# Two orders in a one-core attention and feed-forward kernel: the states' transposes against the tokens' sum, and the PSUM bank of one late product

## The chip, the core and the metric

The kernel runs on one NeuronCore of a Trainium2 chip. The metric is the device time of one execution in microseconds, as the median of several runs. The core has a matrix engine (TensorE; in profiles PE for matmuls and PEld for weight loads), VectorE (DVE), ScalarE (ACT), GpSimd (POOL) and SyncE (SP), which here issues the DMAs. Each engine works through a queue of its own in order and waits on semaphores for the others. SBUF is the working memory; PSUM holds the results of matmuls in eight banks of 128 partitions x 512 float32.

## What is computed

```python
def _attn_ref(x, state):                      # x: (8, 8, 512, 64), state: (8, 8, 32, 64)
    scores = scale * np.matmul(x, state.transpose(0, 1, 3, 2))
    a = softmax(scores)                       # written out: max, exp, sum + 1e-9
    xread = np.matmul(a, state)
    scores2 = scale * np.matmul(state, x.transpose(0, 1, 3, 2))
    a2 = softmax(scores2)
    sread = np.matmul(a2, x)
    return np.concatenate([xread, sread], axis=2)

def _moe_ref(x, w_in, w_out):                 # x: (8 * 544, 512)
    h = x @ w_in                              # 512 -> 2048
    g = h * (1.0 / (1.0 + np.exp(-1.702 * h)))
    return g @ w_out                          # 2048 -> 512
```

The weights of the feed-forward part arrive as float64 and are turned into float32 on the chip. Tokens read the states (`xread`), states read the tokens (`sread`), and the heads are laid side by side as the rows of the feed-forward part.

## The kernel before

The eight batches are handled one after the other. A batch's score products give two sets of exponentials: `e1`, the tokens' over the states, and `e2`, the states' over the tokens. The up product for tokens goes through M, which is the states times `w_in` (`att_M`, one part for each of four column chunks `c`), so that tokens' exponentials times M give `h` directly. The down product is a Strassen scheme of seven products, P1 to P7, each of which is in the middle batches itself a Strassen scheme of seven small ones; the small step `k` of product `P3` is called `P3.k`. VectorE forms the sums and differences that these schemes need, ScalarE copies banks out of PSUM and computes gelu.

The order of all work is written out by hand. While the down product of batch b runs, the attention of batch b + 1 is put between its steps: `hooks_next(b + 1)` fills a table from a step's name to functions, and `strassen_two` calls those of a step when that step's matmuls have been issued. Because every engine's queue is in order, the place in this table sets only the order within each engine. The table serves batches 2 to 7, the middle batches; batches 0 and 1 have their own order.

The piece of it that matters here runs around P3. `x_exp` (ScalarE) makes the tokens' exponentials, in two halves. `x_sum` (VectorE, L573) sums a half of them; `x_inverse` (L577, L578) follows when both sums are there. The states' exponentials `e2` leave for DRAM (`eT_out`) and come back in another layout (`eT_in`, one DMA of 512 KB hooked at P5, into the tile `eT`). `eT_turn(b, i)` (VectorE, L629) transposes one half of `eT` in place: i = 0 covers the head groups j = 0 and 1, i = 1 covers j = 2 and 3. Then `att_sread` (TensorE, L640, hooked at "run", after P3's last product) multiplies `eT` by the tokens, in 32 small matmuls whose innermost index is j. After it come `att_M` for chunks 3 and 2 (L456) and the product P7 (L820). The additions at L825 take a small product of P3 out of its PSUM bank; the first of the two that matter frees the bank into which P3's last small product writes.

At the start the order is another. Batch 0's up products f = 8 to 15 are issued late, by `up_late` through `up_x` and `up` (L673), because they need the last columns of `w_in`. The list `late_banks` gives four of them a bank of their own (`bank_o`). The others take the next bank of the pool `psH` (two buffers, tag "h"), unless `spare` is set, in which case they take the next of the pool `psA` (two buffers, tag "att"). A tile of a pool waits until the readers of the buffer's former tile are done: for `psH` here the gelu on ScalarE (L662). After these products come batch 0's and 1's first down product (L1551), M for batch 1, the states' reads of batches 1 and 0 (L640), an early up product of batch 1, and the down products of batch 0. Pieces of `w_out` are still being converted there: ScalarE clamps exponents (L225, L226), VectorE does the rest (L305 to L322).

The lines that a prediction has to follow in this place are:

```python
def eT_turn(b, i):
    t = A[b]["eT"][:, NG * i : NG * (i + 1)].rearrange("p j g q -> p (j g q)")
    nc.vector.transpose(t, t)

# att_sread: the order of the 32 products
for g in range(NG):
    for c in range(SCH):
        for j in range(NPR):
            e, v = a["eT"][:, j, g, Ns * c : Ns * (c + 1)], xn[b][:, NG * j + g, c]
```

Of the kernel before, what the change touches and what calls it, by code (L numbers as in the profile page):

```python
# [20 lines left out]
def kernel(  # L21
# [39 lines left out]
    NF = DF // P  # L61
# [537 lines left out]
    def att_M(b, c, spare=False, banks=None, copied=True):  # L599

        m = mpool.tile([P, NG, FC], FP32, tag=f"M{turns['M'] % NFC if b < 2 else c}", name=f"M_{b}_{c}")
        turns["M"] += 1
        A[b]["M", c] = m
        name = f"M_{b}_{c}_"
        ps = banks or [
            psH.tile([P, FC], FP32, tag="h", name=name + str(g)) if spare else att_ps([P, FC], name + str(g)) for g in range(NG)
        ]
        by_state(b, ps, lambda rows, j: w_in[c][rows, j])
        M_banks[b, c] = ps
        if copied:  # L610
            M_copies(b, c)
# [52 lines left out]
    def up(key, f, ntok, lhs, rhs, spare=False, bank=None, wait=False, dst=None):  # L664
        if bank is not None:
            hps = bank
        elif spare:
            hps = att_ps([P, ntok], f"h_{key}_{f}")
        else:
            hps = psH.tile([P, ntok], FP32, tag="h", name=f"h_{key}_{f}")  # L670
        n = len(lhs)
        for i in range(n):
            nc.tensor.matmul(hps, lhs[i], rhs[i], start=(i == 0), stop=(i == n - 1))  # L673
        if f % 2 == 0 and dst is None:
            G[key, f // 2] = free.pop(0)
        if dst is None:
            dst = G[key, f // 2][:, f % 2, :ntok]
        waiting.append((nc.scalar.activation, dict(out=dst, in_=hps, func=AF.Gelu_apprx_sigmoid)))
        if not wait:
            gelus(len(waiting))  # L680

    def up_x(b, f, spare=False, bank=None, wait=False, dst=None):
        c, o = divmod(P * f, FC)
        m = A[b]["M", c]
        up(b, f, S, [m[:, g, o : o + P] for g in range(NG)], [A[b]["aT"][:, g] for g in range(NG)], spare, bank, wait, dst)
# [375 lines left out]
    def hooks_next(b):  # L1061

        h = {}

        def at(name, fn, *args):
            h.setdefault(name, []).append((fn, args))

        def att_M1(b):
            att_M(b, 1, banks=[psH.tile([P, FC], FP32, tag="h", name=f"M_{b}_1_0"), bank_o[0]])

        first = b == 2
        p1, p2 = ("P1a", "P2a") if first else ("P1.2", "P1")
        at(p1, att_state, b)
        at(p2, att_scores, b)

        at("P2a" if first else "P2.1", load_x, b)
        at(p2, att_M, b, 0)
        if first:
            at(p2, att_M, b, 1, True)
        else:  # L1080
            at(p2, att_M1, b)
        at(p2, att_blocks, b)
        at("P2a" if first else "P2.1", att_s_max, b)
        p3 = "P2b" if first else "P2.3"
        at("P2a" if first else p3, att_s_exp, b)
        at(p3 if first else "P2", eT_out, b)
        steps = up_sums(b)

        A[b]["sums"] = {0: steps[9:11], 1: [steps[11], steps[14]]}
        if b == 2:  # L1090
            t0, t1, t2, t3 = ((turn_x, (b + 1, i)) for i in range(NPR))
            for i, v in enumerate([[], [t0, t1], [t2, t3]]):
                A[b]["sums"].setdefault(i, []).extend(v)
        elif b + 1 < B:
            for i in range(NPR):
                A[b]["sums"].setdefault(1 + i // 2, []).append((turn_x, (b + 1, i)))
        attention = [
            ("P6.1", att_s_norm), ("P6.1", x_max, 0), ("P6.2", x_sub, 0), ("P6.3", x_exp, 0), ("P6.6", x_max, 1),
            ("P3.1", x_sub, 1), ("P3.3", x_exp, 1), ("P3.4", x_sum, 0), ("P3.5", eT_turn, 0), ("P3.6", eT_turn, 1),
            ("P3.7", x_sum, 1), ("P3.7", x_inverse),  # L1100
            ("P5", eT_in), ("run", att_sread), ("run", att_M, 3, True), ("run", att_M, 2),
            ("T", x_scale, 0), ("T", x_scale, 1), ("P7.5", x_back, 0), ("P7.5", x_back, 1),
        ]
        names = {"P7.6": range(5), "P4.1": (5, 6), "P4.3": (7,), "P4.5": (8,), "P4.6": (12, 13)}
        for name, fn, *args in attention:
            at(name, fn, b, *args)
        for name, n in names.items():
            for i in n:
                at(name, steps[i][0], *steps[i][1])
        at("P7.2", att_srT, b)  # L1110
        return h


    def up_sums(b):

        a = A[b]

        def tt(out, x0, x1, op=ALU.subtract):
            nc.vector.tensor_tensor(out=out(), in0=x0(), in1=x1(), op=op)

        def rooms(step):
            if step == 0:
                t = apool.tile([P, NG, NB, Ns], FP32, tag="e1", name=f"ta_{b}").rearrange("p g i n -> p (g i n)")
                a["T"] = [t[:, QT * i : QT * (i + 1)] for i in range(4)]
            elif step == 1:
                t = apool.tile([P, NPR, S], FP32, tag="xT", name=f"ms_{b}")
                a["S1"], a["S2"] = t[:, :2], t[:, 2:]
            else:
                t = apool.tile([P, NG, SCH, P], FP32, tag="eT", name=f"m4_{b}")
                a["S4"] = t.rearrange("p g c q -> p g (c q)")  # L1130

        def T(i):
            return lambda: a["T"][i]

        def R(g, i):
            return lambda: a["aT"][:, g, QT * i : QT * (i + 1)]

        def M(c, g):
            return lambda: a["M", c][:, g]

        def V(name, c):
            return lambda: a[name][:, c]

        steps = [(rooms, (0,))]
        steps += [(tt, v) for v in ((T(0), R(0, 1), R(0, 0)), (T(2), R(1, 1), R(0, 1)), (T(1), R(1, 1), T(0)), (T(3), R(1, 0), T(1)))]
        steps.append((rooms, (1,)))
        for c in range(2):
            steps.append((tt, (V("S1", c), M(2 + c, 0), M(2 + c, 1), ALU.add)))
            steps.append((tt, (V("S2", c), V("S1", c), M(c, 0))))
            steps.append((tt, (M(2 + c, 0), M(c, 0), M(2 + c, 0))))  # L1150
        steps.append((rooms, (2,)))
        steps += [(tt, (V("S4", c), M(c, 1), V("S2", c))) for c in range(2)]
        return steps
# [153 lines left out]
    nper = FC // P  # L1307
# [122 lines left out]
    late_banks = [None, bank_o[2], None, bank_o[3], bank_o[0], bank_o[1], None, None]  # L1430

    def up_late(f, wait=True):
        up_x(0, f, bank=late_banks[f - 2 * nper], wait=wait)

    for i in range(3):
        up_late(2 * nper + i)
    att_M(0, 3)
    pair_mask(9)
    pair_clamp(9)
    up_late(2 * nper + 3)  # L1440
    up_late(3 * nper)
    round_pair(8, lambda: pair_fraction(9))
    for b in (1, 0):
# [227 lines left out]
    for b in range(1, B):  # L1671
# [21 lines left out]
        if b + 1 < B:  # L1693
            hooks = hooks_next(b + 1)
        else:

            steps, left, right = sr_sums()
            order = (
                ("P5.6", 2), ("P6.1", 3), ("P6.3", 6), ("P6.4", 7), ("P7.5", 8), ("P7.6", 9), ("P4.1", 16, 17), ("P4.5", 18, 19),
            )  # L1700
            hooks = {name: [steps[i] for i in n] for name, *n in order}
            hooks["P3.7"] = [(low_third, (T1,))]
            beside = steps[10:16] + [(low_third, (t,)) for t in (B11, B21, T2, T3, T4, B22)]
            ahead["P2.1"] = [steps[i] for i in (0, 1)]
            ahead["P2.3"] = [steps[i] for i in (4, 5)]
# [46 lines left out]
```

## Time and profile before

| | |
|---|---|
| median of 3 runs | 688.47 us (688.31 to 688.59) |
| the profiled execution | 688.53 us |
| its span, first to last instruction | 686.7 us |
| PE busy | 677.1 us, 99% |
| PEld busy | 578.0 us, 84% |
| DVE busy | 554.9 us, 81% |
| ACT busy | 321.1 us, 47% |
| mean granted TensorE clock | 0.999 |

A profile's timeline has one line for a run of like instructions: start, duration in us, engine, source line, operation, the tile written and those read, their shapes, and how many. A bracket at the end gives the idle time of that engine just before and what ended it. A tile's buffer number is left out of its name: `h` is a bank of `psH`, `sr` the bank of the states' read, `e` the exponentials, `low` and `later` rooms of the Strassen schemes.

### The profile page before, as it was taken

To read this page: it belongs to the slowest core of one execution; us is meant where nothing else is said; L and a number is where in the kernel's file an instruction comes from. 1 tells how busy PE (TensorE), PEld (TensorE's weight loads), DVE (VectorE), ACT (ScalarE), POOL (GpSimd) and SP (SyncE) were. 2 spreads that over 40 slices of the span, in tenths; PEclk is the share of its full clock that TensorE was granted. 3 is DMA by queue.
4 is the path that set the end of the run, shared out by engine and by line. 5 is a ranking of instruction groups with operands and counts; after the bars stand their busy time and mean duration, and the time that the engine had idled before them with its cause. 6 is when DMAs were issued, how large, how long until landed. Compare 5 with 4: busy or idle time off the path is not lost.

```text
span 686.7 us, 13512 instructions
## 1 busy us (share of the span) xinstructions
PE 677.1 (99%) x5339; PEld 578.0 (84%) x5339; DVE 554.9 (81%) x996; ACT 321.1 (47%) x697; POOL 1.5 (0%) x10
## 2 busy tenths in 40 slices
PE   8999999999999999999999999999999999999996
PEld 4443687779988989889988998899988998999995
DVE  5999899999999786988878896888698885986540
ACT  7799543143355534752375335544375237421410
POOL 0000000000000000000000000000000000000000
PEclk9999999999999999999999999999999999999999
DMA  9733446348161754166434645175415640251000
GB/s 319 301 122 93 155 158 145 117 140 273 65 176 55 227 167 110 28 179 190 141 65 125 199 141 110 32 211 189 115 27 169 189 151 1 76 169 48 1 2 30
DMA packets 98526, 89.48 MB, mean 130 GB/s; under 512 B 56736, under 2 KB 77728, under 8 KB 98464
## 3 DMA queue, kind: packets, MB, share of 16 engines
q1 hardware_dynamic: 97920, 88.50, 43.1%
q8 instruction: 42, 0.69, 0.4%
q14 instruction: 20, 0.16, 0.1%
q10 hardware_dynamic: 544, 0.13, 0.1%
HBM read 69.99 MB, written 18.61 MB: 129 GB/s over the span
## 4 chain that ended last, share of the span: by engine, by line
PE 92%; DMA 2%; ACT 2%; DVE 2%; issue 0%; DVEq 0%
PE low L820 28%; PE o L1230 15%; PE o L820 15%; PE upx L1230 6%; PE o L1551 4%; PE M L456 4%; PE h L673 3%; PE down L1551 3%; PE o L719 3%; PE upw L1230 2%; PE o L869 2%; PE o L673 1%; PE down_up L673 1%; PE sr L640 1%; PE o L456 1%; PE upx_sr L1230 1%
## 5 line engine op out<-in xcount | busy, mean ns | idle before, releaser
L820 PE MATMUL low<-w_out,g_room 128*128 128x128 f32 x416 | 54.3, 276 | 0.0
L820 PEld LDWEIGHTS low<-w_out,g_room 128*128 128x128 f32 x416 | 50.5, 192 | 4.5 <-issue 4.2
L1230 PE MATMUL o<-ta,M 128*128 128x256 f32 x192 | 49.9, 382 | 0.0
L1230 PE MATMUL upx<-aT,M 128*128 128x256 f32 x192 | 49.3, 379 | 0.0
L820 PE MATMUL low<-low,g_room 128*128 128x128 f32 x336 | 43.3, 275 | 0.0
L1230 PEld LDWEIGHTS o<-ta,M 128*128 128x128 f32 x192 | 35.5, 190 | 6.0 <-ACT g_room L1276 1.6
L820 PEld LDWEIGHTS low<-low,g_room 128*128 128x128 f32 x336 | 40.3, 192 | 0.0
L1230 PEld LDWEIGHTS upx<-aT,M 128*128 128x128 f32 x192 | 36.0, 190 | 4.6
L1236 ACT ACTIVATE g_room<-o 128x512 f32<-128x512 f32 (+1 forms) x56 | 31.3, 560 | 10.4 <-PE o L1230 10.4
L820 PE MATMUL low<-sums,later 128*128 128x128 f32 x272 | 34.9, 275 | 0.0
L597 ACT COPY M<-M 128x512 f32<-128x512 f32 x53 | 27.6, 596 | 15.1 <-PE M L456 15.1
L820 PEld LDWEIGHTS low<-sums,later 128*128 128x128 f32 x272 | 32.7, 192 | 0.1
L876 DVE TENSOR_TENSOR g_room<-g_room 128x512 f32<-128x512 f32 x48 | 31.8, 686 | 0.2
L1230 PE MATMUL o<-ta,ms 128*128 128x256 f32 x120 | 30.8, 379 | 0.0
L225 ACT ACTIVATE low<-low,edge 128x1024 f32<-128x1024 int32 (+1 forms) x18 | 19.1, 1064 | 21.2 <-DVE low L305 18.2
L1276 ACT COPY g_room<-o 128x512 f32<-128x512 f32 (+1 forms) x28 | 15.6, 556 | 25.3 <-PE o L1230 25.3
L1236 ACT ACTIVATE g_room<-g_room 128x512 f32<-128x512 f32 (+1 forms) x28 | 16.8, 600 | 20.8 <-DVE g_room L1239 20.8
L1230 PEld LDWEIGHTS o<-ta,ms 128*128 128x128 f32 x120 | 22.8, 190 | 3.1
L1230 PE MATMUL o<-aT,m 128*128 128x256 f32 x96 | 24.6, 379 | 0.0
L820 PEld LDWEIGHTS o<-w_out,g_room 128*128 128x128 f32 x160 | 19.4, 192 | 5.0 <-issue 5.0
L456 PE MATMUL M<-w_in,stT 64*32 64x512 f32 x344 | 23.2, 592 | 0.0
L876 DVE TENSOR_TENSOR g_room<-g_room,later 128x512 f32<-128x512 f32 x35 | 22.8, 684 | 0.0
(321 smaller groups left out, 1623.1 us busy)
## 6 DMA issues: line engine op xcount, KB each, us to landing
low<-low SPq DMA_DIRECT2D x108, 256.0 KB, 2.7
low<-low SPq DMA_DIRECT2D x11, 768.0 KB, 5.7
later<-in_moe_w_out_dram SPq DMA_DIRECT2D x16, 512.0 KB, 5.1
w_out<-in_moe_w_in_dram SPq DMA_DIRECT2D x12, 512.0 KB, 10.9
xsq<-in_x_dram SPq DMA_DIRECT2D x96, 64.0 KB, 2.2
xn<-in_x_dram SPq DMA_DIRECT2D x12, 512.0 KB, 4.2
squares<-e SPq DMA_DIRECT2D x32, 128.0 KB, 3.0
eT<-squares SPq DMA_DIRECT2D x8, 512.0 KB, 4.5
```

The source lines that it names most:

```text
L225: nc.scalar.activation(out=sc.bitcast(FP32), in_=sc, func=AF.Relu, bias=edge[0], scale=-8.0)
L456: nc.tensor.matmul(ps[g][st], state_of(b, NG * j + g, g), rhs(rows, j), start=True, stop=True)
L597: nc.scalar.copy(A[b]["M", c][:, g], ps)
L673: nc.tensor.matmul(hps, lhs[i], rhs[i], start=(i == 0), stop=(i == n - 1))
L719: nc.tensor.matmul(ps[:, r], lhs[f][:, P * r : P * (r + 1)], rhs[:, f], start=(first and r == 0 and f == 0), stop=(f == HF - 1), skip_grou ...
L820: nc.tensor.matmul(ps, lhs[f], rhs[:, f], start=(first and f == 0), stop=(f == QF - 1), skip_group_check=True)
L869: nc.tensor.matmul(ps[:, r], lhs[f][:, P * r : P * (r + 1)], rhs[:, f], start=(r == 0 and f == 0), stop=(f == HF - 1), skip_group_check=True,)
L876: nc.vector.tensor_tensor(out=out, in0=x0, in1=x1, op=op)
L1230: nc.tensor.matmul(ps[:, k], lhs[i][:, o : o + P], rhs[i], start=(first and k == 0 and i == 0), stop=(i == n - 1), skip_group_check=True,)
L1236: nc.scalar.activation(out=dst, in_=src, func=AF.Gelu_apprx_sigmoid)
L1276: nc.scalar.copy(c12, Y(u))
L1551: nc.tensor.matmul(ps7[name][:, HN * r : HN * (r + 1)], lhs[:, P * r : P * (r + 1)], rhs, start=(i == 0 and r == 0), stop=(i == HF - 1), s ...
```

## The change

In `hooks_next`, three entries of the table change places: at P3.4 the first transpose of `eT` stands where the sum of the tokens' first half stood, at P3.5 the second transpose where the first stood, and at P3.6 that sum where the second transpose stood. In `up_late`, the product f = 14 (`NF - 2`) sets `spare`, so that it takes a bank of `psA` and no longer one of `psH`. Later tiles of both pools take the other buffer than before. No instruction of computation is added or taken away.

```diff
@@ hooks_next
         attention = [
             ("P6.1", att_s_norm), ("P6.1", x_max, 0), ("P6.2", x_sub, 0), ("P6.3", x_exp, 0), ("P6.6", x_max, 1),
-            ("P3.1", x_sub, 1), ("P3.3", x_exp, 1), ("P3.4", x_sum, 0), ("P3.5", eT_turn, 0), ("P3.6", eT_turn, 1),
+            ("P3.1", x_sub, 1), ("P3.3", x_exp, 1), ("P3.4", eT_turn, 0), ("P3.5", eT_turn, 1), ("P3.6", x_sum, 0),
             ("P3.7", x_sum, 1), ("P3.7", x_inverse),
@@ up_late
     late_banks = [None, bank_o[2], None, bank_o[3], bank_o[0], bank_o[1], None, None]
 
     def up_late(f, wait=True):
-        up_x(0, f, bank=late_banks[f - 2 * nper], wait=wait)
+        up_x(0, f, f == NF - 2, late_banks[f - 2 * nper], wait)
```

## The prediction

> **What bounds the kernel now.** I read the page's head, its busy shares and its chain of work first, then TensorE's waits, then timelines around the two edited places.
>
> ```profile
> span 686.7 us, 13512 instructions
> PE 677.1 (99%) x5339; PEld 578.0 (84%) x5339; DVE 554.9 (81%) x996; ACT 321.1 (47%) x697; POOL 1.5 (0%) x10
> ...
> PE 92%; DMA 2%; ACT 2%; DVE 2%; issue 0%; DVEq 0%
> ```
>
> TensorE's queue is the bound: 99% busy, 92% of the chain. So the change is worth what it takes off that queue at places where nothing else comes due, and no more. Two small waits lie there. First the states' read of a middle batch (number 3), VectorE and then the weight loads:
>
> ```profile
> 246.41 0.68 DVE L573 TENSOR_REDUCE sm<-e 128x16 f32<-128x512 f32 x1
> 247.51 0.29 DVE L825 TENSOR_TENSOR later<-low,later 128x128 f32<-128x128 f32 x1 [0.41 <-PE low L820]
> 247.72 0.70 DVE L629 STREAM_TRANSPOSE eT<-eT 128x512 f32<-128x512 f32 x1
> 248.40 0.29 DVE L825 TENSOR_TENSOR later<-o,later 128x128 f32<-128x128 f32 x1
> 248.79 0.71 DVE L629 STREAM_TRANSPOSE eT<-eT 128x512 f32<-128x512 f32 x1
> 249.43 0.65 DVE L573 TENSOR_REDUCE sm<-e 128x16 f32<-128x512 f32 x1
> ...
> 249.12 0.14 PEld L640 LDWEIGHTS sr<-xn,eT 128*32 128x32 f32 x4
> 249.56 0.93 PEld L640 LDWEIGHTS sr<-xn,eT 128*32 128x32 f32 x60 [0.30 <-DVE eT L629]
> ```
>
> The 32 products of the read leave two records each. Two products (j = 0, 1) need only the first transpose; the third (j = 2) needs the second, which ends at 249.50, and TensorE arrived at 249.12. Batches 0 and 1, whose transposes end early (before 74.7), show the undisturbed read:
>
> ```profile
> 74.99 1.10 PE L640 MATMUL sr<-sums,eT 128*32 128x64 f32 x64
> 75.91 1.08 PE L640 MATMUL sr<-xn,eT 128*32 128x64 f32 x64
> 76.92 1.13 PE L1551 MATMUL o<-w_out,sums 128*128 128x256 f32 x4
> ```
>
> Second, batch 0's late up products:
>
> ```profile
> 62.86 5.42 PE L673 MATMUL o<-aT,M 128*128 128x512 f32 x12
> 67.97 0.60 ACT L662 ACTIVATE sums<-h 128x512 f32<-128x512 f32 x1
> 68.62 3.70 PE L673 MATMUL h<-aT,M 128*128 128x512 f32 x8 [0.34 <-ACT sums L662]
> ```
>
> Product f = 14 takes the bank that f = 8 filled, and stands until f = 8's gelu (67.97 to 68.57) has read it.
>
> **What the skill says.** "PSUM — Partial Sum Buffer", section "Engine vs sequencer instructions": matmuls start and complete in program order, and VectorE's and ScalarE's queues are strict FIFO. So a matmul that waits holds all behind it; the trace agrees, the 60 loads stand behind the third product. The same page, "PSUM bank collisions raise a hardware error": guard PSUM by bank, not by address; so f = 14 must wait for its own bank's reader and for no other, as the 0.34 us shows. "Perfetto Trace Analysis", "Per-engine timelines": a matmul's reported end is estimated and its start lies after its semaphores; I therefore count from start to start.
>
> **The change part by part: the transposes.** VectorE's order at P3.4 to P3.7 of batches 2 to 7 was sum 0, add, transpose 0, add, transpose 1, sum 1; it becomes transpose 0, add, transpose 1, add, sum 0, sum 1. The same six instructions, 0.68 against 0.70 us each: VectorE's work is unchanged and sum 1 ends within some 0.1 us of where it did (the add before it waits for TensorE in both). Nothing is added to a DMA queue; the load of eT stays at P5, ahead of other work on SP. TensorE has as many waits on VectorE as before (one goes from the read's first product, one comes to P7's first product for the second add, done at 248.69 and needed at 252.45).
>
> The second transpose moves up by one place, to end at about 248.4, where transpose 0 ends now: 0.7 us ahead of TensorE in batches 3 to 7, 0.5 in batch 2. The wait goes whole. Its price, start to start from the trace's single records: undisturbed, the third product starts 0.080 us after the first. In batches 2 to 7 it starts 0.320, 0.440, 0.249, 0.249, 0.247 and 0.247 after it. Less 0.080 that is 0.240, 0.360 and four times 0.168, 1.27 together; the restart after each wait costs another 0.024 (a spacing of 60 ns in place of 36), 0.14 for six. Sum 1.41 us. Bounds: 1.27, if that spacing stays; above, from batch 4's whole read, 1.26 to the next start against batch 0's 1.01 (another kind of work follows there), which is 0.25 in place of 0.19, so 1.41 + 6 x 0.06 = 1.77. I take 1.41: same kind of record, same pattern.
>
> What is late next? VectorE runs on without idling to 256.89 and isn't moved. TensorE's next needs of it are P7's second product at 253.45 (its left operand is done at 251.9) and P4's at 259.8 (255): over 1.4 us of room against a gain of at most 0.38. At 257.40 VectorE waits for TensorE again (0.51 us), so from there it follows. ScalarE's copies in between all wait for TensorE and move with it. The gain stays, and adds up from batch to batch.
>
> **The change: f = 14.** It takes a bank of the other pool, last held by batch 0's M product and copied out by 64.43. f = 15 then takes f = 8's bank, free at 68.57, and starts about 69.83. Without a wait f = 14 starts one ordinary spacing (0.429) after the last product at 67.687, at 68.116 and not at 68.622: 0.506. The first spacing after a stop is 0.534 where others are 0.429: another 0.105. Sum 0.61 us. Rotation shifts by one bank in both pools: M_3 of batch 1 gets its first bank free of f = 14's gelu and its second bound to f = 15's (72.35 after the move, needed at 73.39); batch 0's read takes f = 14's bank (its gelu ends by 71.5, needed at 75.3). None waits.
>
> What is late next here: batch 0's eT lands at 73.34 by its own clock and its transposes end at 74.65; TensorE would want them at 74.91 (the read's loads begin 0.39 ahead of its products, at 75.52, less 0.61): 0.26 us of room, the tightest place. Then ScalarE's clamp follows a gelu that waits for TensorE, and VectorE, busy without a break from 82.99 to beyond 134, starts when the clamp ends:
>
> ```profile
> 79.80 0.60 ACT L662 ACTIVATE xn<-h 128x512 f32<-128x512 f32 x1 [2.23 <-PE h L673]
> 80.60 1.17 ACT L225 ACTIVATE low<-low,edge 128x1024 f32<-128x1024 int32 x1
> 81.81 1.15 ACT L226 ACTIVATE low<-low,edge 128x1024 int32<-128x1024 f32 x1
> 82.99 1.22 DVE L318 SCALAR_TENSOR_TENSOR low<-later,low 128x1024 int32<-128x1024 int32 x1 [1.51 <-ACT low L226]
> ```
>
> So that stretch shifts too, out of its 1.51 us of idling. I take 0.61; low end 0.3, if eT lands 0.3 us late.
>
> **Sum.** 1.41 + 0.61 = 2.02 us off the profiled execution: span 686.7 to 684.7, time 688.53 to 686.51. The three runs' median is 688.47, 0.06 below the profiled one: 686.45, in round numbers 686.4.
>
> **Rivals.** (a) The read alone gains: f = 14's 0.61 us is caught again at 74.7 or in VectorE's unbroken stretch. For it: 0.26 us of room, and VectorE without a break from 82.99 on. Against: VectorE's start there hangs on TensorE. 688.47 - 1.41 = 687.1. (b) The reads' gain is handed back: TensorE comes earlier and waits at its next meeting with VectorE. For it: VectorE idles only 0.51 us before 257.40. Against: the rooms above. Then 0.61 is left: 687.9. (c) Slower: eT hasn't landed when transpose 0 now heads VectorE's queue. Behind it stands the first add, which frees the bank of P3's last product, so each us of lateness costs TensorE about one, six times over. In batch 4 eT is issued at 312.50; the median landing is 4.5 us later, 317.0; the transpose would start at 321.23, 4.2 us after. It decides from there: slower by 0.2% needs (1.4 + 2.0) / 6 = 0.57 us of lateness per batch, a landing 9.3 us after issue. At one us: 688.47 - 2.02 + 6 = 692.4.
>
> **How the numbers follow.** A measurement of this kernel tells about 0.2%, 1.4 us, from nothing. The likeliest case (0.68) has its own range from 1.77 + 0.61 to 1.27 + 0.51: 686.1 to 686.7. A part of one gain lost, or (a), 0.17: 686.7 to 687.3, two thirds of it beyond 0.2%. (b) and less, 0.09: 687.3 to 688.6. (c) 0.04. The rest is 0.02 of more gain. Range 685.9 to 687.5. Faster 0.79, within 0.2% 0.16, slower 0.05.
>
> **What would show it.** Right: no idle before the read's 60 loads in batches 2 and 3, its start-to-start time about 1.07 us in all six; no wait ahead of f = 14, which starts at 68.1; VectorE's idle at the clamp about 0.9 us; batch 7's read starts about 1.8 us earlier. Wrong: a VectorE wait on eT's load; a wait of TensorE at 74.9, at P7 or P4; a read that still shows its gap.

## The result, and the profile after

The changed kernel takes 686.27 us (median of 7 runs, 685.89 to 686.4) against 688.58 us for the kernel before: 2.31 us less, a ratio of 0.9966 with a 95% interval of 0.9955 to 0.9978. The profiled execution of it took 686.15 us, 2.38 less than that of before.

The head of the page of the changed kernel, for the lines of the page shown of before:

```profile
span 684.3 us, 13511 instructions
PE 675.0 (99%) x5339; PEld 577.3 (84%) x5339; DVE 554.8 (81%) x996; ACT 320.8 (47%) x697; POOL 1.5 (0%) x10
...
PE 95%; DMA 2%; DVE 2%; ACT 0%; issue 0%; DVEq 0%
```

TensorE is still the bound, and busy for 2.1 us less with the same 5339 matmuls, so the busy time of before had counted most of what the waits cost. TensorE's share of the chain rises from 92 to 95%.

The states' read of batch 3, VectorE and then the weight loads, in the timeline of the changed kernel:

```profile
245.45 0.70 DVE L629 STREAM_TRANSPOSE eT<-eT 128x512 f32<-128x512 f32 x1
246.55 0.29 DVE L825 TENSOR_TENSOR later<-low,later 128x128 f32<-128x128 f32 x1 [0.39 <-PE low L820]
246.76 0.70 DVE L629 STREAM_TRANSPOSE eT<-eT 128x512 f32<-128x512 f32 x1
247.44 0.29 DVE L825 TENSOR_TENSOR later<-o,later 128x128 f32<-128x128 f32 x1
247.83 1.28 DVE L573 TENSOR_REDUCE sm<-e 128x16 f32<-128x512 f32 x2
...
248.16 0.94 PEld L640 LDWEIGHTS sr<-xn,eT 128*32 128x32 f32 x64
```

The second transpose ends at 247.46, 0.70 us ahead of the read's start at 248.16. The 64 loads are one unbroken run where before 4 stood ahead of an idle stretch and 60 behind it. Both sums follow back to back, and VectorE waits for nothing here that it did not wait for before.

The undisturbed reads of batches 1 and 0 and the late products, in TensorE's timeline of the changed kernel:

```profile
62.83 5.42 PE L673 MATMUL o<-aT,M 128*128 128x512 f32 x12
68.08 3.60 PE L673 MATMUL h<-aT,M 128*128 128x512 f32 x8
71.51 1.03 PE L1551 MATMUL o<-w_out,g_room 128*128 128x256 f32 x4
...
74.35 1.10 PE L640 MATMUL sr<-sums,eT 128*32 128x64 f32 x64
75.27 1.08 PE L640 MATMUL sr<-xn,eT 128*32 128x64 f32 x64
```

f = 14 starts at 68.08 with no idle before it. The next work, L1551, starts at 71.51, where it started at 72.16. Laid product against product, the two traces tell where the time went. TensorE is 0.035 us early before f = 14 (from the start of the kernel, which varies), 0.647 after it, and then loses nothing and gains nothing until the read of batch 2. Each of the six reads adds a step, and between the reads the lead stays within 0.04 us:

| read of batch | start to next work before, us | after, us | gain |
|---|---|---|---|
| 2 | 1.337 | 1.031 | 0.306 |
| 3 | 1.457 | 1.031 | 0.426 |
| 4 | 1.268 | 1.031 | 0.237 |
| 5 | 1.266 | 1.031 | 0.235 |
| 6 | 1.264 | 1.031 | 0.233 |
| 7 | 1.265 | 1.031 | 0.234 |

The gains sum to 1.67 us; with 0.61 from f = 14 (0.647 less 0.035) that is 2.28, and with the 0.035 of the start 2.32, against spans 2.4 apart.

### The profile page after: what moved, and what is told of

It is laid out like the page before. It is cut to its first block, busy times and chain, and to the rows that moved or that the text cites. A ratio compares the mean times of both kernels' runs of the same rounds, so it can differ in the third digit from the quotient of the medians.

```text
span 684.3 us, 13511 instructions
## 1 busy us (share of the span) xinstructions
PE 675.0 (99%) x5339; PEld 577.3 (84%) x5339; DVE 554.8 (81%) x996; ACT 320.8 (47%) x697; POOL 1.5 (0%) x10
## 4 chain that ended last, share of the span: by engine, by line
PE 95%; DMA 2%; DVE 2%; ACT 0%; issue 0%; DVEq 0%
PE low L820 28%; PE o L1230 15%; PE o L820 15%; PE upx L1230 6%; PE o L1551 4%; PE h L673 4%; PE M L456 4%; PE down L1551 3%; PE o L673 3%; PE o L719 3%; PE upw L1230 2%; PE o L869 2%; PE down_up L673 2%; PE o L456 1%; PE sr L640 1%; PE upx_sr L1230 1%
```

## Experiments

The kernel before had a median of 688.67 us on the chip of the first four experiments and 688.41 us on that of the last three. My theory was that two waits of TensorE, one for the second transpose and one for f = 8's reader, are the whole of it. The rivals: VectorE being through earlier, the other rotation of the banks, the sum ahead of the transposes as such, and a gain that is handed back at the next meeting of the engines.

**The table alone.**

```diff
-("P3.4", x_sum, 0), ("P3.5", eT_turn, 0), ("P3.6", eT_turn, 1),
+("P3.4", eT_turn, 0), ("P3.5", eT_turn, 1), ("P3.6", x_sum, 0),
```

> The kernel before with the three table entries exchanged and batch 0's late products untouched. Theory (the wait of the read's third product is the whole of this part): each read of batches 2 to 7 takes 1.03 us from start to start as in the changed kernel, against 1.337, 1.457 and four times 1.27, so 1.67 us come off: 686.9 us, and f = 14 keeps its 0.34 us wait. Rival (the two parts hang together, and one alone is caught again at the next meeting with VectorE): less than half of that, 687.7 us or more.

Measured 686.96 us, ratio 0.9976 (0.9967 to 0.9984): 1.71 less than before. All six reads take 1.03 us, and TensorE's waits still list f = 14's (waits of TensorE; in columns the total, the number, the longest):

```profile
PE h L673 <- ACT sums L662: 0.4, 1, 0.4
```

The lead grows at the reads and nowhere else. The part stands on its own.

**f = 14 alone.**

```diff
-        up_x(0, f, bank=late_banks[f - 2 * nper], wait=wait)
+        up_x(0, f, f == NF - 2, late_banks[f - 2 * nper], wait)
```

> The kernel before with f = 14 in the other pool and the table untouched. Theory: f = 14 starts at 68.1, 0.61 us come off there and stay to the end: 687.97 us; the reads keep their gaps. Rival (VectorE, busy without a break from 83 to beyond 134 us, hands it back): the shift shows at 72 us and is gone by 150 us: 688.5 us.

Measured 687.93 us, ratio 0.999 (0.9984 to 0.9997): 0.74 less. TensorE's timeline:

```profile
62.87 5.42 PE L673 MATMUL o<-aT,M 128*128 128x512 f32 x12
68.13 3.60 PE L673 MATMUL h<-aT,M 128*128 128x512 f32 x8
71.56 1.03 PE L1551 MATMUL o<-w_out,g_room 128*128 128x256 f32 x4
```

The reads stay at 1.336, 1.459 and four times 1.265. The trace's lead is 0.60 us at 69 us, and only once, at 385 us, does it move again, by 0.04. So it was not handed back in VectorE's unbroken stretch. The two parts alone sum to 1.71 + 0.74 = 2.45 by the clock and 1.67 + 0.61 = 2.28 by the traces, against 2.31 together: they add up, as far as runs of this spread can tell.

**The first transpose ahead of the sum, the second where it was.**

```diff
-("P3.4", x_sum, 0), ("P3.5", eT_turn, 0), ("P3.6", eT_turn, 1),
+("P3.4", eT_turn, 0), ("P3.5", x_sum, 0), ("P3.6", eT_turn, 1),
```

> The kernel before with P3.4 first transpose, P3.5 sum of the first half, P3.6 second transpose: the first transpose goes ahead of the sum, the second stays where it was. Theory (only the second transpose is late): the gaps in the reads stay at 0.24 to 0.43 us beyond the undisturbed read and the time is that of before, 688.5 us. Rival (the sum ahead of the transposes is what costs, each transpose moved brings its half): 687.7 us.

Measured 688.63 us, ratio 1.0 (0.9991 to 1.0008). The weight loads of batch 3:

```profile
249.30 0.14 PEld L640 LDWEIGHTS sr<-xn,eT 128*32 128x32 f32 x4
249.74 0.93 PEld L640 LDWEIGHTS sr<-xn,eT 128*32 128x32 f32 x60 [0.30 <-DVE eT L629]
```

The same 0.44 us to the third product as before. The first transpose was never late; the sum ahead of it costs nothing by itself. The whole of the table's part is the second transpose.

**f = 15 in the other pool, and not f = 14.**

```diff
-        up_x(0, f, bank=late_banks[f - 2 * nper], wait=wait)
+        up_x(0, f, f == NF - 1, late_banks[f - 2 * nper], wait)
```

> The kernel before with f = 15 and not f = 14 in the other pool; later tiles of both pools change buffers just as in the changed kernel. Theory (the price is f = 14's wait for f = 8's reader): f = 14 still waits 0.34 us and starts at 68.6, 688.5 us. Rival (the other rotation of the later tiles brings the gain): f = 14 waits, and 0.6 us come off after 70 us: 687.9 us.

Measured 688.56 us, ratio 0.9999 (0.9991 to 1.0007). TensorE's timeline:

```profile
68.90 3.70 PE L673 MATMUL h<-aT,M 128*128 128x512 f32 x8 [0.38 <-ACT sums L662]
```

f = 14 waits as it did, and nothing is gained after it. The other rotation of the later tiles is worth nothing; the wait is all.

**The second transpose one place later.** VectorE does the same work in the same stretch; only the last transpose and the last sum change places.

```diff
-("P3.4", x_sum, 0), ("P3.5", eT_turn, 0), ("P3.6", eT_turn, 1),
-("P3.7", x_sum, 1), ("P3.7", x_inverse),
+("P3.4", x_sum, 0), ("P3.5", eT_turn, 0), ("P3.6", x_sum, 1), ("P3.7", eT_turn, 1),
+("P3.7", x_inverse),
```

> The kernel before with the second transpose of batches 2 to 7 moved one place the other way, behind the sum of the second half (P3.7: sum 1, transpose 1, inverse); VectorE has the same work and its chain ends at the same time. Theory (TensorE waits for the second transpose): each read's third product starts about 0.63 us later still, 6 x 0.63 = 3.8 us, 692.4 us (691.5 to 693). Rival (the gain came from VectorE being through earlier): 688.6 us.

Measured 692.01 us, ratio 1.0049 (1.0032 to 1.0066): 3.6 us more. The weight loads of batch 4:

```profile
325.19 0.14 PEld L640 LDWEIGHTS sr<-xn,eT 128*32 128x32 f32 x4
326.03 0.93 PEld L640 LDWEIGHTS sr<-xn,eT 128*32 128x32 f32 x60 [0.69 <-DVE eT L629]
```

The third product now stands 0.84 us behind the start. The reads take 1.930, 2.049 and four times about 1.858, each 0.59 more than before, which is the start-to-start time of the sum that was put ahead (324.69 to 325.28). 6 x 0.59 = 3.6. VectorE's last sum and last transpose of batch 4, in its timeline:

```profile
324.69 0.67 DVE L573 TENSOR_REDUCE sm<-e 128x16 f32<-128x512 f32 x1
325.28 0.70 DVE L629 STREAM_TRANSPOSE eT<-eT 128x512 f32<-128x512 f32 x1
```

That the place of the second transpose in VectorE's queue sets the time is now shown in both directions, and "VectorE is through earlier" falls: in batch 7 its chain from the first add to the inverse took 2.31 us, against 2.40 before, and the kernel was slower all the same.

**The load of eT later, under the changed order.** The changed kernel, with one more edit:

```diff
-            ("P5", eT_in), ("run", att_sread), ("run", att_M, 3, True), ("run", att_M, 2),
+            ("P6", eT_in), ("run", att_sread), ("run", att_M, 3, True), ("run", att_M, 2),
```

> The changed kernel with the load of eT issued at P6 and no longer at P5, behind the three loads of the next right operand; in batch 4 about 316.8 us instead of 310.6, landing about 321.4 where the first transpose would start at 319.85. Theory (with the transposes at the head, a late landing stands in front of the add that frees the bank of P3's last product): VectorE waits about 1.5 us for the load, TensorE about 0.8 us at that last product, six times: 691 us (689.5 to 693), and the stall lies before the read, not in it. Rival (room enough, or the stall is caught again): 686.3 us.

Measured 690.26 us (688.92 to 692.7, a wide spread), some 4 us more than the changed kernel; the ratio to the kernel before is 1.0029 (1.0019 to 1.0039). The first transpose of batch 2 and then TensorE's products there, in the timeline:

```profile
173.81 0.71 DVE L629 STREAM_TRANSPOSE eT<-eT 128x512 f32<-128x512 f32 x1 [1.55 <-DMA eT<-squares]
174.45 0.25 DVE L825 TENSOR_TENSOR later<-low,later 128x128 f32<-128x128 f32 x1
...
172.22 1.06 PE L820 MATMUL o<-w_out,spare_M 128*128 128x128 f32 x8
174.75 1.16 PE L820 MATMUL low<-low,g_room 128*128 128x128 f32 x8 [1.48 <-DVE later L825]
175.84 1.10 PE L640 MATMUL sr<-xn,eT 128*32 128x64 f32 x64
```

The mechanism is the one named: the load is late, the transpose stands at the head of VectorE's queue, the add behind it frees a bank late, and TensorE stops ahead of the read, whose own time stays 1.031 us. The size was wrong in most batches. I expected VectorE to wait 1.5 us and TensorE 0.8 in each. In the profiled execution (689.47 us) VectorE waited 1.56, 0.38, 0.53, 0.54, 1.70 and 0.43 us in batches 2 to 7, and TensorE stopped only in batches 2 (1.48 us of idle time) and 6 (0.84). From start to start against the changed kernel that cost 1.65 and 1.10 us, and the waits up to 0.54 us cost TensorE nothing. In the changed kernel VectorE idles some 0.4 us before that add in batches 3 to 7 anyway, and not in batch 2. That the median lies in the expected range is therefore partly luck: it was worked out from six equal stops.

**The other remedy: the read's products in another order.** On the kernel before, the products of j = 0 and 1 all come first (in the reads of batches 0 and 1 as well).

```diff
-        for g in range(NG):
-            for c in range(SCH):
-                for j in range(NPR):
+        for half in range(2):
+            for g in range(NG):
+                for c in range(SCH):
+                    for j in range(NG * half, NG * half + NG):
```

> The kernel before with the read's 32 products in another order, all of head groups j = 0 and 1 first, then those of j = 2 and 3; the transposes stay where they were. 16 products lie ahead of the first that needs the second transpose, and it ends 0.19 to 0.39 us after the read's start. Theory (the wait is one of that data alone): no idle on the second transpose, 1.67 us less, 686.9 us, if products of two column groups stream as fast as of four. If they don't, the read is longer and its spacing shows by how much; the wait must be gone in either case. Rival (the place in VectorE's queue is what counts): gaps as before, 688.6 us.

Measured 692.33 us, ratio 1.0055 (1.004 to 1.007): slower by 3.9 us. The read of batch 3, TensorE's timeline:

```profile
250.72 1.79 PE L643 MATMUL sr<-xn,eT 128*32 128x64 f32 x64
252.44 1.09 PE L456 MATMUL M<-w_in,stT 64*32 64x512 f32 x16
```

The wait is gone, with the transposes where they were: the read's idle time no longer names VectorE, and no two records stand more than 0.074 us apart until the last. So the wait is one for that half of the data, at the third product. But the read takes 1.725 us in place of 1.031. Each head group j writes its own 32 of the bank's 128 partitions (these are the column groups of the expectation). Where j runs over all four groups, two products come every 56 ns; where it alternates between two, mostly one, and two again only in a short stretch around the change of halves. That costs more than the wait did: 0.46 us per read in batches 4 to 7 (1.725 against 1.27), 0.39 in batch 2, 0.27 in batch 3, and about 1.2 us in the two first reads together. My expectation left this open and named the spacing to look at. Why two groups stream at half the rate was not tried.

## Why the prediction was right

**The sum.** Predicted 686.4 us; measured 686.27. Faster by 2.0 was forecast, 2.31 came.

**The transposes.** The step "the wait goes whole" holds: the second transpose ends 0.70 us ahead of the read in batches 3 to 7 and 0.53 in batch 2, as worked out. The step "third product starts 0.080 after the first" holds to the nanosecond: the first records of the changed reads are 6, 7, 7 and 60 ns apart, as in batch 1. What was undersized is the price of the restart. I took 1.41 us and the reads gave 1.67, within the bound of 1.77. The missing 0.26 is 0.043 per read at its other end: I had forecast 1.07 us for a read, and it took 1.031. Before the change the last two products of the read stood 48 to 50 ns apart ahead of M's first product, and now 6 to 7. I had looked at the start of the read only, and put the difference to batch 0's read down to the other kind of work that follows. That this pair closes up with the wait gone is shown. What holds it apart was not tried; the reordered read has the same two wide spacings, 73 ns between its first two products and 49 between its last two, without any wait, so the wait is not their only cause.

**f = 14.** Predicted start 68.116, gain 0.61; measured 68.08 in an execution that ran 0.035 ahead, gain 0.61. That the stop costs the next spacing as well (0.105) is shown by the difference between 0.506 and the 0.61 that arrived.

**What is late next.** Nothing was, and this is what rivals (a) and (b) would have needed. For (b) it was close: VectorE's idle time ahead of its next wait for TensorE in batch 3 (256.89 to 257.40 before, 0.51 us) shrank to 0.09 us (255.93 to 256.02), as that read gained 0.43 us, more than the 0.38 that I had called the most. In the other batches 0.22 to 0.29 us are left. As for (a), f = 14 alone gives 0.60 us of which all but some 0.05 last to the end, so VectorE's unbroken stretch is not a bound; it shifts with the clamp, which ends at 82.3 and not at 83.0:

```profile
81.16 1.15 ACT L226 ACTIVATE low<-low,edge 128x1024 int32<-128x1024 f32 x1
...
82.34 1.22 DVE L318 SCALAR_TENSOR_TENSOR low<-later,low 128x1024 int32<-128x1024 int32 x1 [1.78 <-ACT low L226]
```

These are ScalarE's and VectorE's timelines of the changed kernel. VectorE's idle time there was forecast at 0.9 us and is 1.78. The start is where it should be; VectorE was done earlier, because batch 0's eT landed at 72.42 and not at 73.34. The step that took 73.34 as a fixed time "by its own clock" was wrong: in the nine profiles, of kernels that all issue this load at the same point of the program, the transpose behind it starts between 72.4 and 74.1.

The room of 0.26 us at batch 0's read was misread as well. I let the read's weight loads begin at 75.52, 0.39 ahead of its products. In the timeline of the kernel before they begin at 75.86, 0.06 ahead:

```profile
75.86 0.97 PEld L640 LDWEIGHTS sr<-xn,eT 128*32 128x32 f32 x64
```

So the room was 0.60 us (75.86, less 0.61, less 74.65), and by either figure a landing 0.3 us late would have cost next to nothing: my low end of 0.3 for this part did not follow. Nor is it a constant: in the profile of the changed kernel the transposes end at 73.72 and the loads begin at 75.21. The latest landing of the nine came 6.35 us after its issue. In the changed kernel, which issued the load at 67.60, the second transpose would then end at about 75.25 (an estimate from these traces), where the third product's weights begin to load at 75.27: no room would be left. No profile of the changed kernel fell there.

**Rival (c)**, a late load at the head of VectorE's queue, is real where the load is made late. My price of about one us per us of lateness was met only in batch 2, where VectorE does not idle ahead of the add (1.65 us lost for a wait of 1.56); batch 6 lost 1.10 us for 1.70, and waits of 0.38 to 0.54 us cost nothing. With the load at P5 no wait for it appears in the changed kernel's batches 2 to 7.

## What to carry to other kernels

Where one engine is the bound, lay its records start to start against an undisturbed instance of the same work: the differences here were 0.23 to 0.61 us each, and they added up to the whole gain. The profile's idle times showed them in part (0.34 of 0.61 us, 0.30 of 0.43) or, in four of the six reads, not at all. A wait is mended by the one instruction that is late: moving the second transpose up by one place was worth the table's whole part, moving the first alone nothing. Before bringing a consumer of a load forward, look at what its queue holds behind it, and how far the landing varies from run to run.

## What was not expected of the hardware

- A read cost more than its third product was late. In batches 4 to 7 that product started 0.17 us late, with 73 ns in place of 7 between the two products ahead of it, and the read took 0.235 us longer: behind the wait one spacing was 60 ns in place of 36, and the last pair stood 49 apart in place of 7. Why is open.
- 32 small products (128 x 32 weights, 64 columns) whose outputs run over four groups of 32 partitions took 1.031 us; the same products, alternating between two groups, 1.725.
- A 512 KB load from DRAM (batch 0's eT), issued at the same point of the program, landed between 4.8 and 6.4 us after its issue over the nine profiles, as the start of the transpose behind it tells.
